# Scores of six chunks by their heads' rows, a switch for the causal mask of four chunks, and another order of the opening

## The chip, the cores and the metric

The kernel runs on one core of a Trainium2 chip. The metric is the device time of one launch in microseconds (us), as a median of several runs. The engines of the core are TensorE (PE), VectorE (DVE), ScalarE (ACT), GpSimd (POOL) and SyncE (SP), which issues the transfers. Each engine works through its own list of instructions in order.

## The reference

Two parts follow one another. The first is a recurrence with gates over 4 batches, 8 heads and 768 tokens, with heads of 40 numbers; its output, scaled by an output gate, is the input of the second, a feed-forward layer (FFN) on 3072 tokens of 320 numbers.

```python
for t in range(S):                                  # B, H, S, D = 4, 8, 768, 40
    m_new = np.maximum(f_gate[:, :, t] + m, i_gate[:, :, t])
    f_stab = np.exp(f_gate[:, :, t] + m - m_new)
    i_stab = np.exp(i_gate[:, :, t] - m_new)
    C = f_stab * C + i_stab * outer(vt, kt)         # one 40 x 40 state for each batch and head
    n = f_stab * n + i_stab * kt
    y[:, :, t] = sigmoid(o_gate) * (C @ qt) / np.maximum(np.abs(n @ qt), 1.0)
x = y.transpose(0, 2, 1, 3).reshape(3072, 320)
h = x @ w_in                                        # w_in 320 x 2048
g = np.maximum(h, 0.0) + alpha * np.minimum(h, 0.0)
out = g @ w_out                                     # w_out 2048 x 320
```

The weights `w_in` and `w_out` are stored as 64-bit floats.

## The kernel before

The tokens are cut into 24 chunks of 128. Within a chunk the recurrence is computed in closed form: products of q and k (the scores, `pS`), multiplied by the decay between the two tokens (`E`, zero where the second token is later than the first), times v (`pH`), plus what the state `C` of the chunks before gives (`pI`). A chunk's result, scaled by the gate (`og`, `xn`), is transposed to `x`. Two chunks make a group, and each of the 12 groups runs through the FFN: eight steps up (`ph`, 16 products each), a relu with slope on ACT and DVE (`g`), a split into a high part (`gh`, ACT) and a low part (`gl`, DVE or POOL), and eight steps down (`po`).

Chunks 0 to 5 are treated in another way than the rest. They make the opening, in which the weights are also fetched and turned from 64 bits into two parts of 32 bits each, high (`WH`, `OH`, `W`) and low (`WL`, `OL`). The opening ends when the first group's output is copied from `po` to `ob`. Behind it a written pattern of steps repeats for all further groups.

The order of the opening is written out by hand in the string `ORDER`. Each word is a step; the steps issue their instructions in this order, and `pin()` ties every engine, the queue of transfers on SP among them, to just this order. The words that matter here:

- `dq4`, `dv1`, `do1`, `dL4`: SP fetches q and k of chunk 4, v of chunks as stated, output gates, decay rows. Their tiles are `qn`, `kn`, `va`, `og`, `Lb`. The tiles of q and k are two each and serve the chunks by turns, so the load for chunk 4 needs chunk 2's transposes to be done.
- `qT4 qc4`, `kT4 kc4`: PE transposes q or k of chunk 4 into `pqk`, ACT copies it to `qf` or `kf`.
- `sp31`: PE spreads the decay of chunk 3's odd heads over a bank `pb` (L1064); `ex31`: ACT takes the exponential into `E`. `barred` (L100) adds, ahead of the spreading, a product with the mask `later`. `sc31`: the scores; `wg31`: DVE weighs them (L1101). `v3`: the product with v. `um3 uc3`: update of `C` (L221, L222). `gr3 gg3 gx3 gp3`: the gate (L439) and the product with it (L443).
- `i21d s x j h l`: a block of `w_in` (column block 2, row block 1; `wi2_1`); `d` loads it, `s` makes the upper bits on ACT (L855), then either `x` (one more pass on ACT, L865, and `j`, a join on DVE, L877) or `y` (a shift on DVE, L871, and `j`, L879). `h` is the high part on ACT (L887), `l` the low part on DVE and `p` the same on POOL (L891). `r` stands for the rest of `w_in` (`wr`), `o` for a block of `w_out` (`wo`).
- `U00 R00 S00 G00 K00` and `V01 r01 s01 g01 N01`: step up, relu, slope, high part, low part; with the capital letters DVE takes the low part, with V, small letters and N POOL does. `D00` is the step down, `Z0` the copy of the group's output.

Before, the scores of a chunk were computed for even and odd heads apart (`sc30`, `sc31`). A head's 40 rows lie at partitions 0 to 39 or 64 to 103 of the tiles. The products took all 104 rows, so the rows of the other head had to be zero in one operand: `kf` has two halves, each filled for one parity alone and set to zero elsewhere by four POOL memsets at the start.

```python
nc.tensor.matmul(ps[:, sl], qk[n][1][:R, par, sl], qk[n][0][:R, sl], start=True, stop=True)   # R = 104
```

Of the kernel before, what the change touches and what calls it, by code (L numbers as in the profile page):

```python
# [17 lines left out]
def kernel(ctx: ExitStack, tc: tile.TileContext, q, k, v, i_gate, f_gate, o_gate, w_in, w_out, alpha, out):  # L18
# [286 lines left out]
    kpads = []  # L305

    def padded_tiles():


        for K in kpads:  # L310
            nc.gpsimd.memset(K[64:R, 0], 0.0)
            nc.gpsimd.memset(K[:64, 1], 0.0)

# [3 lines left out]

    def padded(n):
        return kpads[(n + NDIR) % 2]

    def padded_copy(K, pk):
        nc.scalar.copy(K[:64, 0], pk[:64])
        nc.scalar.copy(K[64:R, 1], pk[64:R])
# [92 lines left out]
    def gated_steps(n, hv):  # L416
# [63 lines left out]
    def decays_of(n, par, Lb):  # L480

        b, c = divmod(n, NC)
        E = sb.tile([P, 512], F32, tag="E", name=f"E{n}_{par}", bufs=4)
        for p in range(NPR):
            h = 2 * p + par
            nc.scalar.activation(  # L486
                E[:, p * P : (p + 1) * P], Lb[:, h], AF.Exp, bias=bT[:, c, b * H + h : b * H + h + 1]
            )
        nc.gpsimd.affine_select(
            out=E, in_=E, pattern=[[0, NPR], [1, P]], base=0, channel_multiplier=-1,  # L490
            compare_op=ALU.is_ge, fill=0.0,
        )
        return E
# [162 lines left out]
    def first_stacks():  # L656
# [23 lines left out]
    XNP = range(2, NBF)  # L680
    KDP = range(1, 24)
    CP = range(6, 24)
    OBA = range(0)
    WIDE = 3 * VA
    ORDER = """warm18 kfz alT lf0z warm2 warm2 i00d i00s sca0 lf0a lf0b dq0 L0 sp01 qT0 dq1 alC li0 bj0 wt0 bTt kT0 i00x qc0 kc0 ewj
        i01d sca1 bTc ex01 sp00 sc00 qT1 wTt eeL wTc qc1 wd0 li1 lf1a lf1b kT1 sc01 i00j ex00 kc1 eTt Cz eTc sp11 ex11
        dv0 wg01 i01s wd1 L1 um0 uc0 i01x lpa um1 sp10 wg00 gma gmd ex10 i01j i00h fm1 ft1 sc11 do0 sc10 wg10 bj1 wtl
        blt ewl blc i00p o0d o0s r0d o0x gmm gmc r0s r0x v0 wg11 lpb lpc lpd uc1 dq2 qT2 o2d gr0 wlt og1 warm2 wlc r0j
        i11d lpe o0j i01h i01p gg0 qc2 dq3 gx0 gp0 kT2 v1 eel elt elc sp21 kc2 sc21 dL r0H ta1 gr1 gg1 sp20 ex21 qT3
        wg21 i10d dv1 r0h gx1 gp1 r0p r0L ex20 wd2 sc20 wg20 qc3 x0 x1 xa0 xd0 dq4 fm2 wd3 xa1 xd1 i10s F0 ft2 o2s o2y  # L690
        sp31 o0h ex31 kT3 o2j o2h i10y i10j um2 U00 o0l V01 kc3 R00 i11s uc2 i11y i11j o2l do1 i10h i10l sp30 r01 qT4
        qc4 ex30 S00 v2 sc31 i20d i20s ta2 gr2 i20x wg31 o1d og2 gg2 gx2 kT4 i20j kc4 sc30 wg30 G00 K00 i21d fm3 ft3
        s01 i20h o1s i20p i11h i11p o1x r2d o1j i21s i21x sc41 v3 um3 i21j uc3 ta3 dL4 U02 V03 r2s r2y o3d gr3 sc40
        ex41 fm4 R02 dq5 o1h o1l o4d g01 r2j N01 qT5 i21h i21p o3s S02 o3x G02 K02 dL5 wg41 i31d ft4 D00 wd4 dq6 o3j
        qc5 dv2 r2h r2p r03 ex40 o4s r2H D01 o4x gg3 s03 o3h o4j gx3 o5d gp3 wg40 i30d V04 r04 s04 dv3 o4h V05 gp2 x2
        x3 xa2 xd2 o6d do2 wd6 kT5 g04 r2P g03 o3l xa3 r05 o4l s05 v4 xd3 kc5 i31s ta4 N03 N04 i31y i31j i30s o5s o5x
        F1 V10 gr4 r10 um4 uc4 dL6 i30x um6 U11 ex50 R11 o5j s10 uc6 S11 ex51 g10 i31h dL7 i31p sc50 N10 i30j dq7 wg50
        U12 fm5 ft5 o5h sc51 wg51 v5 o7d R12 S12 ta5 D10 G11 K11 o6s o6x gr5 og3 gg5 G12 gx5 gg4 D11 K12 D12 i30h i30l
        gx4 U13 gp5 D02 tp0 do3 U06 o7s gp4 o5l o6j vp0 R13 tp1 g05 S13 G13 N05 K13 o7x o6h D13 vp1 o7j U07 tp2 tp3
        R06 S06 R07 x4 x5 xa5 xd5 D03 D04 D05 S07 o7h o7l G06 K06 o6l D06 xa4 xd4 G07 K07 D07 Z0"""  # L700
# [36 lines left out]
    class FeedForward:  # L737

        def __init__(self, g):
            self.g, self.x, self.done, self.named = g, x_tiles.pop(g), [], 0  # L740
# [4 lines left out]
        def up(self):  # L745
            for step in self.up_steps(self.g < 2):
                pass

        def up_steps(self, split=True):
            g, fp = self.g, self.named  # L750
            self.named += 1
# [34 lines left out]
            self.done.append((gh, gl))  # L786
# [179 lines left out]
    def first_group():  # L966
# [79 lines left out]
        def spread(n, par):  # L1046

            pb = psa(f"pb{n}_{par}")
            barred(pb)
            for p in range(NPR):  # L1050
# [3 lines left out]
                    start=False, stop=p == NPR - 1  # L1054
# [3 lines left out]
        def spread_later(n, par):  # L1058

            pb = psa(f"pb{n}_{par}")  # L1060
            barred(pb)
            for p in range(NPR):
# [3 lines left out]
                    LP[:, n % GC * P : (n % GC + 1) * P], start=False, stop=p == NPR - 1,  # L1066
# [5 lines left out]
        def decay(n, par):  # L1072
# [10 lines left out]
            E[n, par] = e  # L1083
# [4 lines left out]
        def scores(n, par):  # L1088
            if n >= GC:
                ps = psa(f"pS{n}_{par}")  # L1090
            elif n * par == 0:
                ps = ps_h.tile([P, 512], F32, tag="h", name=f"pS{n}_{par}")
            else:
                ps = ps_o.tile([P, 512], F32, tag="o1", name=f"pS{n}_{par}")
            for p in range(NPR):
                sl = slice(p * P, (p + 1) * P)
                nc.tensor.matmul(ps[:, sl], qk[n][1][:R, par, sl], qk[n][0][:R, sl], start=True, stop=True)
            pS[n, par] = ps
# [94 lines left out]
        def later_decays():  # L1193
# [29 lines left out]
            kfz=padded_tiles, Cz=zero_states,  # L1223
# [12 lines left out]
        def chunk_steps(n):  # L1236
# [61 lines left out]
        def named_ffn(g):  # L1298
# [68 lines left out]
```

## Time and profile before

| what | us |
|---|---|
| median of 3 runs (lowest, highest) | 465.4 (465.05, 465.82) |
| the profiled execution | 465.35 |
| its span | 463.6 |
| first group's output copied out from | 104.20 |

The profile is that of one execution; its span lies inside that execution's time, and 1.75 us lie around it. The engines' busy times are sums over all instructions; matmuls overlap each other, and their ends are modelled, so a busy PE may still lose time from one matmul's start to the next. A row of a group gives the line and the tiles, out<-in, with sizes, the count, the busy time and mean duration, and the idle time in front of them. A row of a timeline starts with the start time and the duration of a run of like instructions.

### The profile page before, as it was taken

Reading aid. Unit: us, or ns where it says so; the run is one execution under the profiler, and the core shown is the slowest. Engines: PE = TensorE matmul, PEld = TensorE weight load, DVE = VectorE, ACT = ScalarE, POOL = GpSimd, SP = SyncE. Lnnn points to the kernel's source line nnn. Section 1 sums busy time; section 2 is a strip of 40 time slices with the busy share of each in tenths; the row PEclk is TensorE's granted clock in tenths of the full one; section 3 lists DMA queues with packets and bytes.
Section 4 is the critical chain, followed back from the end, with each engine's and each line's share of the span. In section 5 each row is a group of like instructions: output and inputs, shape, how many; then the busy total and the mean of one; then the engine's idle time right before and its main releaser. Section 6 shows DMA issues by size and latency. Waiting matters only on the chain.

```text
span 463.6 us, 11813 instructions
## 1 busy us (share of the span) xinstructions
PE 452.8 (98%) x4366; PEld 442.0 (95%) x4366; DVE 329.8 (71%) x692; ACT 315.0 (68%) x707; POOL 308.4 (67%) x377
## 2 busy tenths in 40 slices
PE   8989989999999999999999999999999999999996
PEld 6879978999999999999999999999999999999996
DVE  4989998747776787886875887886776786764321
ACT  4899898676857858758856958757857858423331
POOL 8551674854698697588888598588888686324231
PEclk9999999999999999999999999999999999999999
DMA  9999994869775775888997686688796463020000
GB/s 184 177 221 252 277 252 118 175 122 190 151 182 147 138 184 160 137 174 173 158 187 176 122 197 168 133 166 180 153 206 156 107 154 90 1 84 15 28 2 28
DMA packets 186306, 68.67 MB, mean 148 GB/s; under 512 B 150234, under 2 KB 178506, under 8 KB 186250
## 3 DMA queue, kind: packets, MB, share of 16 engines
q1 hardware_dynamic: 186170, 67.83, 67.2%
q8 instruction: 34, 0.56, 0.5%
q14 instruction: 22, 0.18, 0.2%
q10 hardware_dynamic: 80, 0.11, 0.1%
HBM read 40.44 MB, written 7.57 MB: 104 GB/s over the span
## 4 chain that ended last, share of the span: by engine, by line
PE 83%; DVE 5%; DMA 5%; SPq 3%; ACT 3%; issue 1%; ACTq 0%; DVEq 0%
PE po L796 36%; PE ph L759 5%; PE ph L765 5%; PE ph L762 5%; PE ph L760 5%; PE ph L761 5%; PE ph L764 4%; PE ph L763 4%; PE ph L766 4%; PE pH L377 4%; PE pS L515 4%; DMA wi<-in_moe_w_in_dram 2%; DMA wr<-in_moe_w_in_dram 2%; PE pI L403 1%; PE pu L203 1%; DMA qn<-in_q_dram 1%
## 5 line engine op out<-in xcount | busy, mean ns | idle before, releaser
L785 POOL TENSOR_TENSOR gl<-g,gh 128x512 fp32r<-128x512 f32 x77 | 100.5, 1306 | 42.9 <-ACT gh L783 39.6
L796 PE MATMUL po<-OH,gh 128*128 128x320 f32 x368 | 110.7, 312 | 0.0
L796 PE MATMUL po<-OL,gh 128*128 128x320 f32 x368 | 109.3, 309 | 0.0
L769 ACT ACTIVATE g<-ph 128x512 f32<-128x512 f32 x96 | 57.1, 596 | 58.2 <-PE ph L766 56.0
L774 DVE SCALAR_TENSOR_TENSOR g<-g,oma,ph 128x256 f32<-128x256 f32 x156 | 66.8, 469 | 32.7 <-ACT g L769 32.3
L796 PEld LDWEIGHTS po<-OL,gh 128*128 128x128 f32 x368 | 69.2, 188 | 0.1
L796 PEld LDWEIGHTS po<-OH,gh 128*128 128x128 f32 x368 | 69.1, 188 | 0.0
L796 PE MATMUL po<-OH,gl 128*128 128x320 f32 x368 | 69.0, 309 | 0.0
L759 PE MATMUL ph<-XH,WH 128*128 128x256 f32 x192 | 57.2, 298 | 1.1 <-ACT wo L865 0.7
L796 PEld LDWEIGHTS po<-OH,gl 128*128 128x128 f32 x368 | 57.9, 188 | 0.0
L764 PE MATMUL ph<-XL,WH 128*128 128x256 f32 x192 | 54.3, 283 | 0.9 <-DVE XL L623 0.9
L765 PE MATMUL ph<-XL,WH 128*128 128x256 f32 x192 | 54.3, 283 | 0.0
L762 PE MATMUL ph<-XH,WL 128*128 128x256 f32 x192 | 54.3, 283 | 0.0
L760 PE MATMUL ph<-XH,WH 128*128 128x256 f32 x192 | 54.1, 282 | 0.0
L761 PE MATMUL ph<-XH,WL 128*128 128x256 f32 x192 | 54.1, 282 | 0.0
L364 ACT CAST E<-pS 128x512 bf16<-128x512 f32 x72 | 41.6, 582 | 18.0 <-DVE pS L361 14.0
L763 PE MATMUL ph<-XH,W 128*128 128x256 f32 x192 | 53.4, 278 | 0.2 <-POOL W L891 0.2
L766 PE MATMUL ph<-XL,W 128*128 128x256 f32 x192 | 53.4, 278 | 0.0
L783 ACT CAST gh<-g 128x512 fp32r<-128x512 f32 x77 | 46.5, 618 | 9.1 <-DVE g L774 6.6
L486 ACT ACTIVATE E<-Lb,bT 128x128 f32<-128x128 f32 x160 | 50.0, 392 | 0.0
L361 DVE TENSOR_TENSOR pS<-pS,E 128x512 f32<-128x512 f32 x36 | 24.8, 690 | 29.6 <-PE pS L515 26.2
L759 PEld LDWEIGHTS ph<-XH,WH 128*128 128x128 f32 x192 | 36.1, 188 | 2.0 <-ACT wo L865 0.9
(197 smaller groups left out, 1123.2 us busy)
## 6 DMA issues: line engine op xcount, KB each, us to landing
Lb<-L_d SPq DMA_DIRECT2D x20, 512.0 KB
wo<-in_moe_w_out_dram SPq DMA_DIRECT2D x8, 640.0 KB
wi<-in_moe_w_in_dram SPq DMA_DIRECT2D x8, 512.0 KB
qn<-in_q_dram SPq DMA_DIRECT2D x24, 160.0 KB
kn<-in_k_dram SPq DMA_DIRECT2D x24, 160.0 KB
va<-in_v_dram SPq DMA_DIRECT2D x24, 160.0 KB
og<-in_o_gate_dram SPq DMA_DIRECT2D x24, 160.0 KB
out_dram<-ob SPq DMA_DIRECT2D x11, 320.0 KB
```

What stands on the lines that cost most here:

```text
L759: nc.tensor.matmul(dst, WH[half][:, 0, hs], XH[:, 0], start=True, stop=False)
L760: nc.tensor.matmul(dst, WH[half][:, 1, hs], XH[:, 1], start=False, stop=False)
L761: nc.tensor.matmul(dst, WL[half][:, 0, hs], XH[:, 0], start=False, stop=False)
L762: nc.tensor.matmul(dst, WL[half][:, 1, hs], XH[:, 1], start=False, stop=False)
L763: nc.tensor.matmul(dst, W2[:, fs], X2, start=False, stop=False)
L764: nc.tensor.matmul(dst, WH[half][:, 0, hs], XL[:, 0], start=False, stop=False)
L765: nc.tensor.matmul(dst, WH[half][:, 1, hs], XL[:, 1], start=False, stop=False)
L766: nc.tensor.matmul(dst, W2[:, fs], X2L, start=False, stop=True)
L769: nc.scalar.activation(gt, ph, AF.Relu, scale=-1.0)
L774: nc.vector.scalar_tensor_tensor(out=y[:, e], in0=gt[:, e], scalar=oma[:, f : f + 1], in1=ph[:, e], op0=ALU.mult, op1=ALU.add)
L785: (nc.vector if split else nc.gpsimd).tensor_tensor(gl, y, gh.bitcast(F32), ALU.subtract)
L796: nc.tensor.matmul(po[j], x[:, e, j * P : (j + 1) * P], W[f // NB][:, f % NB], **ends)
```

## The change

There are four parts.

1. `scores(n)` computes all eight heads in one step, each with its own 40 rows, even and odd heads by turns into two banks. The step `sc{n}0` or `sc{n}1` that comes first does it, the other one does nothing. The padded tiles, their memsets and the second copy of k go away.
2. `BAR` names the chunks with a product with the mask; the others get a select on POOL (`causal`). `BAR` is `range(4)`: chunks 0 to 3 keep the product, and chunks 4 and 5 had a select before.
3. Numbers that set which engine takes a step: `OGP` (chunk 0's gate on POOL), `XNP` (chunks whose product with the gate is on POOL: 1 to 3, before 2 to 5), `CP` (chunks whose update of `C` starts on POOL: 1, 3 and 4 are added).
4. Another `ORDER`, and `first_turns`, a list of the two kinds of PSUM bank in the order in which the opening asks for them. In the new order seven of the thirteen blocks that took `x` take `y`, and four low parts `l` of `w_out` and two others become `p`. Two more steps up of group 1 and one of group 0 are written with small letters. The order of the loads is another one.

```diff
-    XNP = range(2, NBF)
-    KDP = range(1, 24)
-    CP = range(6, 24)
+    XNP = range(1, 4)
+    KDP = (1, 2, 3, 4, *range(6, 24))
+    CP = (1, 3, 4, *range(6, 24))
+    OGP = range(1)
+    BAR = range(4)
...
+    def open_gate_early(n):
+        if n in OGP:
+            sg = o_tiles[0][:, n]
+            nc.gpsimd.tensor_scalar(sg, sg, 1.0, None, ALU.add)
...
         if b == 0:
-            nc.vector.scalar_tensor_tensor(out=sg, in0=sg, scalar=1.0, in1=rb, op0=ALU.add, op1=ALU.mult)
+            if n in OGP:
+                nc.gpsimd.tensor_tensor(sg, sg, rb, ALU.mult)
+            else:
+                nc.vector.scalar_tensor_tensor(out=sg, in0=sg, scalar=1.0, in1=rb, op0=ALU.add, op1=ALU.mult)
...
-    def padded_copy(K, pk):
-        nc.scalar.copy(K[:64, 0], pk[:64])
-        nc.scalar.copy(K[64:R, 1], pk[64:R])
...
-                copy(qk[n][j][:R], pq[:R])
-            else:
-                padded_copy(qk[n][j], pq)
+                K = sb.tile([P, 2, 512], F32, tag="kS", name=f"kf{n}", bufs=2)[:, 0]
+                qk[n] = sb.tile([P, 512], F32, tag="qf", name=f"qf{n}"), K
+            copy(qk[n][j][:R], pq[:R])
...
             pb = psa(f"pb{n}_{par}")
-            barred(pb)
+            if n in BAR:
+                barred(pb)
...
-            E[n, par] = e
+            E[n, par] = e if n in BAR else causal(e)
...
+        def scores(n):
+            for par in range(2):
+                if n >= GC:
+                    pS[n, par] = psa(f"pS{n}_{par}")
...
+            for h in range(H):
+                p, par = divmod(h, 2)
+                sl, r = slice(p * P, (p + 1) * P), slice(64 * par, 64 * par + D)
+                nc.tensor.matmul(pS[n, par][:, sl], qk[n][1][r, sl], qk[n][0][r, sl], start=True, stop=True)
...
-                steps[f"sc{n}{par}"] = lambda par=par: scores(n, par)
+                steps[f"sc{n}{par}"] = lambda: (n, 0) in pS or scores(n)
...
-        wg21 i10d dv1 r0h gx1 gp1 r0p r0L ex20 wd2 sc20 wg20 qc3 x0 x1 xa0 xd0 dq4 fm2 wd3 xa1 xd1 i10s F0 ft2 o2s o2y
...
+        sc20 dq4 i20y i11s qT4 S00 sc31 sp30 gr2 i11y r01 qc4 i20j og2 wg31 G00 i11j ga2 r2d fm3
```

Three places show what the order moves. In the rows below a tile has its name and a running number; `qn0` is the tile that q of chunks 2 and 4 shares with chunk 0.

SP's queue before, from the load of chunk 4's q and k (`dq4`: the first two rows) to that of chunk 5's (the last two):

```order
L106 DMA qn0_75<-in_q_dram 128x8x40
L106 DMA kn0_77<-in_k_dram 128x8x40
L135 DMA og0_341<-in_o_gate_dram 128x8x40 x2
L845 DMA wi2_0_665<-in_moe_w_in_dram 128x1024
L928 DMA wo2_676<-in_moe_w_out_dram 128x2x640
L845 DMA wi2_1_699<-in_moe_w_in_dram 128x1024
L845 DMA wr2_719<-in_moe_w_in_dram 64x1024 x2
L126 DMA Lb4_755<-L_d_88 128x8x128
L928 DMA wo6_794<-in_moe_w_out_dram 128x2x640
L106 DMA qn1_76<-in_q_dram 128x8x40
L106 DMA kn1_78<-in_k_dram 128x8x40
```

SP's queue now, down to the load of chunk 4's q and k (the last two rows):

```order
L846 DMA wi1_0_416<-in_moe_w_in_dram 128x1024
L846 DMA wi2_0_457<-in_moe_w_in_dram 128x1024
L846 DMA wi1_1_485<-in_moe_w_in_dram 128x1024
L1264 DMA L_d_88<-g_L_131 32x768
L138 DMA og0_212<-in_o_gate_dram 128x8x40 x2
L846 DMA wi2_1_584<-in_moe_w_in_dram 128x1024
L929 DMA wo2_595<-in_moe_w_out_dram 128x2x640
L109 DMA qn1_76<-in_q_dram 128x8x40
L109 DMA kn1_78<-in_k_dram 128x8x40
L109 DMA qn0_75<-in_q_dram 128x8x40
L109 DMA kn0_77<-in_k_dram 128x8x40
```

Chunk 4's loads stand behind the gate, three weight blocks (`wi2_0`, `wi2_1`, `wo2`) and chunk 5's loads, all of which they had in front of before.

PE before, behind the first two steps up: one spreading, the transposes of chunk 4's q, chunk 2's product with v, and chunk 3's scores, odd heads first:

```order
L1064 MATMUL pb3_0_629<-LP_90,pick_91 128x128
L266 MATMUL pqk4_0_637<-ident_72,qn0_75 104x128 x4
L337 MATMUL pH2_651<-va1_80,E2_0_496 128x126
L337 MATMUL pH2_651<-va1_80,E2_1_476 128x126
L337 MATMUL pH2_651<-va1_80,E2_0_496 128x126
L337 MATMUL pH2_651<-va1_80,E2_1_476 128x126
L337 MATMUL pH2_651<-va1_80,E2_0_496 128x126
L337 MATMUL pH2_651<-va1_80,E2_1_476 128x126
L337 MATMUL pH2_651<-va1_80,E2_0_496 128x126
L337 MATMUL pH2_651<-va1_80,E2_1_476 128x126
L1097 MATMUL pS3_1_660<-qf3_509,kf1_134 128x128 x4
L266 MATMUL pqk4_1_681<-ident_72,kn0_77 104x128 x4
```

PE now, behind the second step up:

```order
L767 MATMUL ph0_1_610<-XL0_519,W2_73 128x256
L274 MATMUL pqk4_0_641<-ident_72,qn0_75 104x128 x4
L1099 MATMUL pS3_0_648<-qf3_483,kf3_482 128x128
L1099 MATMUL pS3_1_649<-qf3_483,kf3_482 128x128
L1099 MATMUL pS3_0_648<-qf3_483,kf3_482 128x128
L1099 MATMUL pS3_1_649<-qf3_483,kf3_482 128x128
L1099 MATMUL pS3_0_648<-qf3_483,kf3_482 128x128
L1099 MATMUL pS3_1_649<-qf3_483,kf3_482 128x128
L1099 MATMUL pS3_0_648<-qf3_483,kf3_482 128x128
L1099 MATMUL pS3_1_649<-qf3_483,kf3_482 128x128
L103 LDWEIGHTS ident_72
L103 MATMUL pb3_0_658<-later_92,ident_72 128x512
```

The eight products of chunk 3 stand together and go to two banks by turns; chunk 2's product with v has moved ahead of the two rows' step up, and the spreading behind the scores.

POOL now, where two low parts of `w_out` (`OL`) stand between low parts of `w_in`, a product with the gate, an update of `C` and a select:

```order
L892 TENSOR_TENSOR OL_105<-t_wo_357,OH_104 128x640
L892 TENSOR_TENSOR WL_103<-t_wi_0_597,WH_102 128x512
L438 TENSOR_TENSOR xn_664<-T_564,og_212 128x320
L892 TENSOR_TENSOR WL_703<-t_wi_0_607,WH_702 128x512
L892 TENSOR_TENSOR WL_103<-t_wi_1_639,WH_102 128x512
L218 TENSOR_TENSOR C_85<-C_87,gamB 104x336
L488 AFFINE_SELECT E_1_802<-E_1_802 128x512
L892 TENSOR_TENSOR OL_105<-t_wo_741,OH_104 128x640
```

Before, the two `OL` were steps of DVE, and so was the product that starts the update of `C`.

More of the change, by code (lines that the diff above doesn't have):

```diff
@@ L40 @@
     turns = ["b", "a"]
+    first_turns = list("abababababaabababbbabaababaabbaabbaabbaababbaababab")
     def psa(name, tag=None):
+        if tag is None and first_turns:
+            tag = first_turns.pop(0)
         if tag is None:
@@ L303, in shifted @@
         chunk[n] = (Q, K, None)
[L305 to L312, printed above, removed]
     def zero_states():
@@ L488, in decays_of, with causal @@
             )
+        return causal(E)
+    def causal(E):
         nc.gpsimd.affine_select(
@@ L739, in __init__ @@
         def __init__(self, g):
-            self.g, self.x, self.done, self.named = g, x_tiles.pop(g), [], 0
+            self.g, self.x, self.done = g, x_tiles.pop(g), {}
             if g == 1:
@@ L743, in __init__, with up_steps @@
                 self.po = [ps_a.tile([P, 512], F32, tag="b", name=f"po{g}_{j}")[:, :DM] for j in range(GC)]
[L745 to L751, printed above, removed]
+        def up_steps(self, fp, split):
+            g = self.g
             XH, XL, X2, X2L = self.x
@@ L1027, in by_token @@
             yield
-        for j in range(2):
-            kpads.append(sb.tile([P, 2, 512], F32, tag="kS", name=f"kf{j}", bufs=2))
         qk = {}
@@ L1053, in spread @@
                     pb[:, p * P : (p + 1) * P], ident[:, h : h + 1].broadcast_to([P, P]), L_all[:, n * P : (n + 1) * P],
-                    start=False, stop=p == NPR - 1
+                    start=n not in BAR, stop=n not in BAR or p == NPR - 1
                 )
@@ L1060, in spread_later @@
             pb = psa(f"pb{n}_{par}")
-            barred(pb)
+            if n in BAR:
+                barred(pb)
             for p in range(NPR):
@@ L1065, in spread_later @@
                     pb[:, p * P : (p + 1) * P], pick[:, h : h + 1].broadcast_to([3 * BH, P]),
-                    LP[:, n % GC * P : (n % GC + 1) * P], start=False, stop=p == NPR - 1,
+                    LP[:, n % GC * P : (n % GC + 1) * P], start=n not in BAR, stop=n not in BAR or p == NPR - 1,
                 )
@@ L1082, in decay @@
                 )
-            E[n, par] = e
+            E[n, par] = e if n in BAR else causal(e)
             yield
         pS = {}
[L1088 to L1098, printed above, removed]
+        def scores(n):
+            for par in range(2):
+                if n >= GC:
+                    pS[n, par] = psa(f"pS{n}_{par}")
+                elif n * par == 0:
+                    pS[n, par] = ps_h.tile([P, 512], F32, tag="h", name=f"pS{n}_{par}")
+                else:
+                    pS[n, par] = ps_o.tile([P, 512], F32, tag="o1", name=f"pS{n}_{par}")
+            for h in range(H):
+                p, par = divmod(h, 2)
+                sl, r = slice(p * P, (p + 1) * P), slice(64 * par, 64 * par + D)
+                nc.tensor.matmul(pS[n, par][:, sl], qk[n][1][r, sl], qk[n][0][r, sl], start=True, stop=True)
         def weigh(n, par):
@@ L1245, in chunk_steps @@
                 add(f"fm{n} ft{n}", lazily(lambda: state_part(n)))
+            steps[f"ga{n}"] = lambda: open_gate_early(n)
             add(f"gr{n} gg{n} gx{n} gp{n}", lazily(lambda: gated_steps(n, got["T" if n else "h", n])))
@@ L1306, in named_ffn @@
                 for tokens, split in (("URSGK", True), ("VrsgN", False)):
-                    add(" ".join(f"{x}{g}{fp}" for x in tokens), lazily(lambda split=split: ffs[g].up_steps(split)))
+                    add(" ".join(f"{x}{g}{fp}" for x in tokens), lazily(lambda fp=fp, split=split: ffs[g].up_steps(fp, split)))
                 steps[f"D{g}{fp}"] = lambda fp=fp: ffs[g].down(fp)
```

42 lines of the change are left out of this document (22 added, 20 removed).

## The prediction

> **What bounds the kernel now.** First the page: the span, then each engine's share.
>
> ```profile
> span 463.6 us, 11813 instructions
> PE 452.8 (98%) x4366; PEld 442.0 (95%) x4366; DVE 329.8 (71%) x692; ACT 315.0 (68%) x707; POOL 308.4 (67%) x377
> ```
>
> PE is busy for 98% of the span, so a gain needs less PE work or fewer of the few microseconds in which PE is idle. The profiled execution took 465.35 us: 463.6 of span and 1.75 around it. The median of the runs, 465.4 us, is the same within 0.05 us, and I add my sum to 465.35. Next the stretches, to see where those few are (PE, weight loads, DVE, ACT, POOL, granted clock, DMA share, GB/s).
>
> ```profile
> 0.00:10.00 10.00, 8.27 (x54) 6.36 (x54) 4.82 (x14) 4.21 (x6) 8.47 (x27) 1.00 0.99 171
> 10.00:20.00 10.00, 9.48 (x106) 8.56 (x104) 7.60 (x13) 8.99 (x28) 6.82 (x9) 1.00 1.00 211
> 20.00:30.00 10.00, 8.42 (x75) 7.32 (x73) 8.93 (x21) 8.63 (x18) 3.92 (x5) 1.00 1.07 241
> 30.00:40.00 10.00, 9.64 (x96) 8.69 (x95) 8.88 (x20) 9.40 (x24) 3.43 (x4) 1.00 0.84 159
> 40.00:50.00 10.00, 9.82 (x96) 9.38 (x96) 9.64 (x19) 9.80 (x21) 3.65 (x3) 1.00 1.09 295
> 34.90:66.00 31.10, 30.03 (x265) 29.02 (x260) 28.49 (x55) 28.43 (x61) 14.72 (x15) 1.00 1.04 261
> 66.00:104.30 38.30, 36.31 (x300) 35.27 (x299) 26.81 (x54) 29.17 (x65) 24.67 (x30) 1.00 0.70 150
> 104.30:463.60 359.30, 355.78 (x3537) 351.72 (x3534) 249.09 (x529) 231.27 (x520) 246.42 (x291) 1.00 0.62 134
> ```
>
> The diff touches only the opening, which ends when the first FFN group is copied out near 104.3 us. Behind that PE is busy for 355.78 of 359.30 us with work that the change leaves as it is, so what the opening gains or loses is carried to the end. In the opening, the DMA share is at 0.99 or above in all but one of the slices to 50 us: up to there transfers set the pace. From 34.9 to 66 PE (30.03 of 31.10), DVE (28.49) and ACT (28.43) are all close to full; PE is idle for 1.07 us there and 1.99 us behind it. The chain of waits says the same of the start:
>
> ```profile
> 14.25 8.14 DMA wr<-in_moe_w_in_dram
> 28.56 4.91 DMA qn<-in_q_dram
> ```
>
> Two transfers and the steps behind them carry the path up to the first up product. PE's own waits name DVE and ACT (total us, times, longest):
>
> ```profile
> PE ph L764 <- DVE XL L623: 0.9, 1, 0.9
> PE pb L100 <- DVE xn L443: 0.8, 1, 0.8
> PE pH L337 <- DVE E L1101: 0.8, 2, 0.6
> PE ph L759 <- ACT wo L865: 0.7, 1, 0.7
> ```
>
> **The scores by their heads' rows.** Before, a chunk's eight products use 104 rows with zeros in one operand; now they use 40 rows, at partitions 0 and 64 by turns, into two banks. PE's timeline of before (start, us, line, operation) has both shapes' nearest relatives:
>
> ```profile
> 17.80 1.99 PE L1097 MATMUL pS<-qf,kf 104*128 104x128 f32 x16
> 19.72 0.43 PE L1022 MATMUL ps_gb<-ident,g_WH 32*128 32x32 f32 x4
> 19.99 0.55 PE L1188 MATMUL pg<-g_gd,unit 32*104 32x192 f32 x2
> 34.51 0.51 PE L203 MATMUL pu<-va,kd 128*40 128x42 f32 x16
> 34.94 0.38 PE L759 MATMUL ph<-XH,WH 128*128 128x256 f32 x1
> 39.28 0.60 PE L266 MATMUL pqk<-ident,qn 128*104 128x128 f32 x4
> ```
>
> A chunk's sixteen records take 19.72 − 17.80 = 1.92 us from start to start, 120 ns each. If two products in different rows run side by side, the floor is half, 0.96 us; another floor is loading 128 columns of weights, which the four records of ps_gb do in 19.99 − 19.72 = 0.27 us, 67 ns each, so 1.08 us for sixteen. The pu products, packed by columns, need 34.94 − 34.51 = 0.43 us for sixteen, 27 ns each, and show that this PE does run neighbours together; they are small, though, so I stay with the nearer row: 1.2 us with the change into and out of the mode, a gain of 0.72 us for a chunk. Ends: 0 (nothing overlaps) and 0.96. Six chunks make 4.3 us, but the first three lie in the stretch that transfers pace; their 2.2 us turn into waiting. Chunks 3 to 5 lie behind: **−2.2 us** (0 to −2.9).
>
> The Trainium skill says on "TensorE: Matmul & The Clock Gate", Part 3 (packing small matmuls), that products in different row groups run together, four such in a third of the time; the same page's section on LDWEIGHTS prices a load by its columns alone, estimated from it 107 ns for 128 of them, which would leave sixteen records at 1.71 us and make the term −0.6 instead of −2.2. The ps_gb row, 67 ns, speaks against that second figure; no row shows row packing itself.
>
> **The mask.** The rows added in the code let a chunk leave out the product with the mask and take a select instead, but the set `BAR` holds chunks 0 to 3, so those keep their products, and 4 and 5 had selects before. POOL's list has as many selects as before. This part costs and brings nothing.
>
> **Work taken from ACT and DVE, put on POOL.** Rows of the opening (busy us, mean ns):
>
> ```profile
> L865 ACT ACTIVATE wo<-wo 128x640 uint32<-128x640 uint32 x7 | 5.6, 806 | 0.0
> L865 ACT ACTIVATE wi<-wi 128x512 uint32<-128x512 uint32 x5 | 3.4, 676 | 0.0
> L322 ACT COPY kf<-pqk 64x512 f32<-64x512 f32 x6 | 3.5, 577 | 0.4 <-PE pqk L266 0.4
> L891 DVE TENSOR_TENSOR OL<-t_wo,OH 128x640 fp32r<-128x640 f32 x8 | 7.0, 891 | 0.0
> L785 DVE TENSOR_TENSOR gl<-ph,gh 128x512 fp32r<-128x512 f32 x4 | 2.7, 683 | 0.7 <-ACT gh L783 0.7
> L221 DVE TENSOR_TENSOR C<-C,gamB 40x168 f32<-40x168 f32 x8 | 2.5, 318 | 0.1
> L871 DVE TENSOR_SCALAR t_wi<-t_wi 128x512 uint32<-128x512 uint32 x3 | 1.7, 574 | 0.0
> L891 POOL TENSOR_TENSOR WL<-t_wi,WH 128x512 fp32r<-128x512 f32 x6 | 8.2, 1371 | 1.6 <-ACT WH L887 1.5
> L785 POOL TENSOR_TENSOR gl<-g,gh 128x512 fp32r<-128x512 f32 x4 | 6.2, 1569 | 2.3 <-ACT gh L783 2.3
> L312 POOL MEMSET kf<- 64x512 f32 x2 | 1.0, 517 | 0.1
> ```
>
> ACT loses seven conversion passes (4 × 0.806 for wo, 2 × 0.676 for wi and one of wr, which has wi's size: 5.3 us) and six of its twelve kf copies (6 × 0.577 = 3.5; the six that stay read 104 partitions instead of 40 or 64): −8.8 us. DVE gains seven shifts in their place (7 × 0.574 = +4.0) and loses four low parts of w_out (4 × 0.891 = 3.6), two of W and WL (priced as gl, 1.4), three gl (2.0) and six half updates of C (1.9): −4.9 us. Chunk 0's gate goes to POOL and one of POOL's gate products comes to DVE, which I count as even for DVE. POOL loses four memsets (2.1) and gets the four low parts of w_out (1.371 × 640/512 = 1.7 each, estimated by size: 6.9), the two of W and WL (2.7), three gl (4.7), three full updates of C and one gate step net, which are smaller than WL's 128×512 and count 0.8 each, as an estimate by size (3.2): about +15 us, with POOL busy for 14.72 of 31.10 and 24.67 of 38.30 us in the two stretches. All this lies beside PE. What it can bring is the removal of waits: PE's idle 1.07 + 1.99 = 3.06 us behind 34.9, of which DVE and ACT are named in each of the rows above. With both relieved I take three quarters away: **−2.3 us** (0 to −3.1).
>
> **Against it, the loads.** The order of the loads on SP's queue changes, and one move matters: q of chunk 4 (qn0, step dq4) stood ahead of a gate load (og) and three loads of weights (wi2_0, wo2, wi2_1); now it stands behind all four and behind chunk 5's q and k. Added up from the order, 8.95 MB are ahead of it and in it; k follows. Before, by the GB/s column, 1.71 + 2.11 + 2.41 + 1.59 = 7.82 MB had moved by 40 us; the other 1.13 MB at 295 GB/s would take 3.8 us more: 43.8 us at the latest. But the slice with 159 GB/s holds an idle queue:
>
> ```profile
> 28.56 2.23 SPq L106 DMA_DIRECT2D qn<-in_q_dram  x1
> 34.22 0.37 SPq L106 DMA_DIRECT2D kn<-in_k_dram  x1
> SPq L106 <- POOL WL L891: 4.7, 1, 4.7
> ```
>
> From 30.8 to 34.2 SP issued nothing, since the load of k waited for POOL. In the new order no load of q or k stands at that place; the slice at 250 GB/s would have moved 0.9 MB more, so 8.95 MB by 40.9 us. I take **42.6** (ends 40.9 and 43.8). PE reached the transposes of chunk 4's q at 39.28 before, 4.3 us behind the first up product at 34.94. Now the value product of chunk 2 stands ahead of them (sixteen records of 112 ns, 1.8 us) and one spreading goes behind (0.6): +1.2 us, moved and not added, so PE gets there at 40.5 if the first up product starts where it did, and stands until 42.6. Scores of chunk 3 and all later up products are queued behind. **+2.1 us** (0.4 to 3.3). The first two chunks' q and k come first now, and v of chunk 1 moves ahead of q of chunk 2: the first up product may start earlier by what PE is idle from 20 us on, 1.58 and at most 0.36 us, or later by 0.8. The later start has two sources. DVE's gate product of chunk 0 now waits for two steps on POOL, and behind it in DVE's queue stand chunk 1's gate, the join of W's rest and chunk 2's weighting, for which the first x transposes and v of chunk 2 wait. And a chunk's scores take two banks at once, so a bank may come free late, as in the row of pb, where PE waited 0.8 us. An earlier start only lengthens the standing at chunk 4, so I count **0** (0 to +0.8).
>
> **Sum.** −2.2 − 2.3 + 2.1 + 0 = −2.4 us; 465.35 − 2.4 = 462.95, say 463.0.
>
> **Rivals.** *No overlap by rows.* If the sixteen records stay at 1.92 us, −2.2 falls away: −0.2, so 465.2. For it speaks that no row of this trace shows packing by rows, against it pu's 27 ns. The skill's LDWEIGHTS price is nearest to this rival.
>
> *POOL in DVE's way.* One pair of rows shows the danger (POOL's timeline, DVE's timeline, DVE's group of the same step):
>
> ```profile
> 52.53 1.76 POOL L785 TENSOR_TENSOR gl<-g,gh 128x512 fp32r<-128x512 f32 x1 [0.99 <-ACT gh L783]
> 53.07 1.77 DVE L879 SCALAR_TENSOR_TENSOR t_wr<-wr,t_wr 128x512 uint32<-128x512 uint32 x1
> L879 DVE SCALAR_TENSOR_TENSOR t_wi<-wi,t_wi 128x512 uint32<-128x512 uint32 x3 | 2.1, 692 | 0.1
> ```
>
> The same join takes 0.69 us elsewhere; beside POOL's subtraction it ended 0.55 us after that did, 1.08 us late. With POOL 15 us busier, five of twelve joins caught like this would cost DVE 5.4 us, more than the 4.9 it is relieved of. Then the −2.3 falls away, and where DVE was already close to full, the excess of 0.5 us comes on top: 465.35 − 2.2 + 2.1 + 0.5 = 465.75. By the Trainium skill, "SBUF — State Buffer", section on who interferes with whom, DVE operations with two SBUF inputs and POOL's reads take one lock in turn, and the loser waits the whole operation; the pair of rows agrees, with 1.08 us.
>
> *The load later still: slower.* If chunk 4's q lands at 46 instead of 42.6, PE stands 3.4 us longer and the sum is +1.0: 466.4. It decides from 45.0 us on, where the sum is zero. For it: transfers of q, k, v and the gates are in small pieces, and the DMA share is at its limit already; against: bytes alone give 43.8 with the old stall.
>
> *Everything in time.* If q lands before 40.5 and the waits go, −2.2 − 3.1 and up to −0.9 from an earlier start: 459.2.
>
> **How the numbers follow.** Chances: my sum 0.40, everything in time 0.17, no overlap 0.15, POOL in DVE's way 0.12, the late load 0.16. The likeliest gives 463.0, with its own range of 461 to 464.5. The runs of before spread by 0.17%, so 0.2%, 0.93 us, is what can be told from no change. Faster: 0.40 × 0.95 + 0.17 + 0.15 × 0.35 = 0.60. Slower: 0.16 and half of POOL's 0.12, with a hundredth for the rest: 0.23. Same: the other 0.17. The range leaves a tenth on either side: from 459.4, inside the best case, to 466.6, just past the late load.
>
> **What would show it.** The sixteen score records in about 1.2 us instead of 1.92 (0 gained if 1.9); PE idle before the transposes of chunk 4's q near 40 to 43 us, released by the transfer of qn; ACT some 9 us less busy before the first copy-out and POOL some 15 more; joins at 0.7 us when free and above 1.2 when caught; the first output copied near 102 instead of 104.2 us. The prediction is wrong if that copy comes later than 103.5, or if the stretch behind it is not 359 us long.

## The result

The changed kernel is slower: 468.78 us (468.4 to 469.08) against 465.23 for the kernel before on the same chip, a ratio of 1.008 with a 95% interval of 1.0068 to 1.0092. A second measurement on another chip gave 469.17 and 1.0090 (1.0072 to 1.0107). The forecast was 463.0 with a range of 459.4 to 466.6. The profiled execution has a span of 466.9 us.

```profile
span 466.9 us, 11801 instructions
PE 454.3 (97%) x4366; PEld 442.0 (95%) x4366; DVE 328.5 (70%) x684; ACT 307.7 (66%) x694; POOL 325.0 (70%) x386
```

ACT is relieved and POOL loaded as forecast. PE's busy time has not shrunk, but it counts records that take longer at a lowered clock, as the next rows show. The stretches of the opening (same columns as before) say where to look:

```profile
10.00:20.00 10.00, 10.00 (x105) 8.82 (x104) 6.67 (x13) 7.54 (x24) 7.00 (x9) 0.83 1.11 242
30.00:40.00 10.00, 9.15 (x99) 8.51 (x96) 8.64 (x17) 7.44 (x17) 6.44 (x7) 1.00 0.96 247
40.00:50.00 10.00, 7.09 (x45) 5.71 (x45) 7.08 (x15) 5.93 (x17) 2.95 (x3) 0.62 1.22 222
50.00:60.00 10.00, 10.00 (x93) 9.68 (x94) 7.26 (x13) 7.74 (x16) 7.22 (x8) 0.87 0.92 259
```

From 40 to 50 us PE is busy for 7.09 us with 45 matmul records, where it had 96 before. And the granted clock, 1.00 in every one of these stretches before, is 0.62 here, 0.87 in the next, and 0.83 from 10 to 20. The waits of PE and its timeline around 40 us:

```profile
PE pqk L274 <- DMA qn<-in_q_dram: 2.9, 1, 2.9
...
PE ps_gb L1023 <- ACT qf L1039: 0.9, 1, 0.9
```

```profile
40.13 0.28 PE L767 MATMUL ph<-XL,W 128*128 128x256 f32 x1
43.32 1.07 PE L274 MATMUL pqk<-ident,qn 128*104 128x128 f32 x4 [2.91 <-DMA qn<-in_q_dram]
44.32 2.08 PE L1099 MATMUL pS<-qf,kf 40*128 40x128 f32 x16
46.33 0.61 PE L103 MATMUL pb<-later,ident 128*128 128x512 bf16 x1
```

PE comes to the transposes of chunk 4's q at 40.4 and starts them at 43.32, when the transfer of `qn`, issued at 35.75, has landed. Then they take 1.07 us for what took 0.60 before, and the scores 2.08. Slices of one microsecond (PE busy, granted clock, DMA share, GB/s) show why:

```profile
41.00:42.00 1.00, 0.00 (x0) 1.00 1.48 136
42.00:43.00 1.00, 0.00 (x0) 0.68 1.51 163
43.00:44.00 1.00, 0.68 (x4) 0.50 1.18 183
...
51.00:52.00 1.00, 1.00 (x6) 0.50 0.69 119
52.00:53.00 1.00, 1.00 (x9) 0.70 0.81 246
53.00:54.00 1.00, 1.00 (x14) 1.00 0.80 274
```

While PE stands idle the granted clock falls from 1.00 to 0.50, and it stays there for nine microseconds after PE is at work again. The first group's output is copied out 3.72 us later than before (104.20), and later than the 103.5 that the prediction had named as the sign of being wrong:

```profile
107.92 0.89 DVE L830 COPY ob<-po 128x320 f32<-128x320 f32 x2 [1.85 <-PE po L797]
```

Span and copy-out moved by about the same, 3.3 and 3.7 us, so the stretch behind the opening is as long as it was: 466.9 − 107.92 = 359.0 us, before 463.6 − 104.20 = 359.4.

The profiled execution of the second measurement has the same place, with other sizes:

```profile
40.00:50.00 10.00, 6.30 (x41) 5.28 (x40) 6.53 (x14) 6.10 (x16) 2.22 (x3) 0.73 1.24 216
PE pqk L274 <- DVE t_wi L880: 3.7, 1, 3.7
```

The load is issued 1.1 us later (36.84), the transposes start at 44.31 after a wait of 3.7 us, and the clock is at half for 6.8 us, from 44.6, just after PE is at work again, to 51.4, and nowhere else. The view puts this wait down to a step of DVE that ended just then; the two loads exchanged, below, show that it is the load.

### The profile page after: what moved, and what is told of

Its sections match the earlier page's. It is cut to its first block, busy times and chain, and to the rows that moved or that the text cites. A ratio compares the mean times of both kernels' runs of the same rounds, so it can differ in the third digit from the quotient of the medians.

```text
span 466.9 us, 11801 instructions
## 1 busy us (share of the span) xinstructions
PE 454.3 (97%) x4366; PEld 442.0 (95%) x4366; DVE 328.5 (70%) x684; ACT 307.7 (66%) x694; POOL 325.0 (70%) x386
## 4 chain that ended last, share of the span: by engine, by line
PE 87%; ACT 3%; POOL 3%; DMA 3%; issue 2%; DVE 1%; SPq 0%; POOLq 0%
PE po L797 36%; PE ph L760 5%; PE ph L763 5%; PE ph L766 5%; PE ph L761 5%; PE ph L762 5%; PE ph L765 5%; PE ph L767 4%; PE ph L764 4%; PE pH L369 4%; PE pS L514 4%; DMA qn<-in_q_dram 2%; PE pu L211 1%; PE pI L395 1%; DMA wi<-in_moe_w_in_dram 1%
## 5 line engine op out<-in xcount | busy, mean ns | idle before, releaser
L786 POOL TENSOR_TENSOR gl<-g,gh 128x512 fp32r<-128x512 f32 x78 | 101.9, 1309 | 37.8 <-ACT gh L784 34.5
L775 DVE SCALAR_TENSOR_TENSOR g<-g,oma,ph 128x256 f32<-128x256 f32 x162 | 69.4, 469 | 32.5 <-ACT g L770 32.2
```

The lines of the kernel that those rows point to most:

```text
L775: nc.vector.scalar_tensor_tensor(out=y[:, e], in0=gt[:, e], scalar=oma[:, f : f + 1], in1=ph[:, e], op0=ALU.mult, op1=ALU.add)
L786: (nc.vector if split else nc.gpsimd).tensor_tensor(gl, y, gh.bitcast(F32), ALU.subtract)
```

## The experiments

All times are medians in us, ratios are against the kernel before, measured beside it on the same chip (464.87 to 465.12). Where single executions are told apart, it is by the mean of their granted clock: 3.41 us at half clock lower it by about 0.004 (3.41 × 0.5 / 463). First the late load was undone, filled, or left with an earlier start.

**Chunk 4's load ahead of two weight blocks.**

```diff
-        o0p ft2 o2j U00 i21d v2 o1d i10s dq5 ...   sc20 dq4 i20y i11s qT4
+        o0p ft2 o2j U00 dq4 i21d v2 o1d i10s dq5 ...   sc20 i20y i11s qT4
```

> The changed kernel with one word of the order moved: the load of chunk 4's q and k stands ahead of the fifth and sixth weight blocks (wi2_1, wo2) and of chunk 5's q and k again. Theory 'late load and clock': PE's 2.9 us wait for that transfer goes, and with it the ten microseconds at half clock behind it, up to 7.9 us in all; some of it turns into waits for DVE and ACT, so 461 to 464 us, with a granted clock of 1.00 from 40 to 56 us. Rival 'POOL's added work': DVE and POOL are what is late in this stretch, the freed time turns into waits for them, and the time stays above 467.5.

Measured 465.36, ratio 1.000 (0.9986 to 1.0014). No trace of it shows the clock; two kernels below that have the load in time do ("Both" and "The two loads exchanged"). The move of one word gives the whole loss back, so POOL's added work is not what made the kernel slower. It does not reach the 461 to 464 that the gain in PE time would have given.

**Idle products in the wait.**

```diff
-        i20y i11s qT4 S00 sc31
+        i20y i11s warm26 qT4 S00 sc31
```

> The changed kernel, with 26 idle products of 256 columns (107 ns each, 2.8 us) put on PE right ahead of the transposes that wait for chunk 4's q. Nothing else moves; the transfer lands as late as it did. Theory 'late load and clock': the wait is filled, the clock stays at 1.00, and up to 5 us (ten microseconds at half clock) come back: 464 to 466.5. Rival 'the wait alone': the half clock lay beside work of DVE and ACT that sets the pace there, and the time stays within 0.8 us of the changed kernel's 468.8.

Measured 467.81, ratio 1.0065 (1.0039 to 1.0091): between the two expectations, and not clearly better than the changed kernel, whose interval it overlaps. In the profiled execution (469.19) the clock stayed at 1.00 from 40 to 60 us, but it fell earlier instead (0.83 from 20 to 30), everything behind was 2 us later, and the load landed at 45.20. The executions differ widely: three with a mean clock of 0.999 or 1.000 took 465.47 to 466.12, the other nine, at 0.996 or less, 467.36 to 471.35. So where the wait was filled and the clock fell nowhere, most of the loss was gone, with the load as late as before; the median does not show it.

**The first copies first.**

```diff
-        alT kT0 warm2 i00s qc0 dv0 li0 lf0b alC i01d kc0 L0
+        alT kT0 warm2 qc0 dv0 li0 lf0b alC i01d kc0 i00s L0
```

> The changed kernel, with ACT's copies of chunk 0's q and k ahead of its first weight conversion, which waits for a transfer until 7.83 us. Both theories: PE's 0.9 us wait at 8 us goes, and the half clock from 11 to 15 us with it (1.9 us of PE time). Theory 'late load and clock': PE only reaches the late load sooner and stands there longer, so the time stays at 467.8 to 469. Rival 'PE paces the start too': 2 us and more come back, 466.8 or less.

Measured 468.37, ratio 1.0063 (1.0042 to 1.0083), as the late load has it: with the load still late, PE waited 3.9 us for it instead of 2.9. What is won ahead of the late load is spent in front of it.

**Both.** The two edits above together, the load's move and the first copies.

> Both edits: chunk 4's load early and the first copies first. Theory 'late load and clock': no half clock anywhere, and what PE gains at the start is no longer lost at the load: 459.5 to 463, at least 1 us below the kernel with the early load alone. Rival 'transfers pace the start': the same as with the early load alone, within 0.6 us.

Measured 465.23, ratio 1.0002 (0.9989 to 1.0015): the same as with the load alone, so the rival held. In the profile, of an execution 0.9 us below the median (464.30), the copy-out starts at 103.17, but PE still waits where DVE and ACT are late. This kernel, with neither long wait, was the ground for the next four.

**All 104 rows again.**

```diff
-                sl, r = slice(p * P, (p + 1) * P), slice(64 * par, 64 * par + D)
+                sl, r = slice(p * P, (p + 1) * P), slice(0, R)
```

> The kernel with both edits (early load, first copies first; 465.2 us), whose scores again take all 104 rows for each of the eight products, so that no two run side by side. The other head's rows are not zero here, so the scores are sums over two heads: only the time counts. It undoes the row packing alone. Theory 'the packing's gain turns into waits': six chunks get 0.8 us longer on PE, of which PE then waits less for DVE, ACT and transfers; 465 to 466.5 us. Rival 'PE paces the opening': the 5 us come back in full, 469 to 470.5.

Measured 464.83, ratio 0.9994 (0.9985 to 1.0004). Taking the packing away costs nothing. The packing itself works; the changed kernel's timeline has a chunk's sixteen records at full clock from 18.29 to the next group at 19.38, 1.09 us instead of 1.92:

```profile
18.29 1.16 PE L1099 MATMUL pS<-qf,kf 40*128 40x128 f32 x16
19.38 1.12 PE L389 MATMUL pI<-C,qf 104*128 104x126 f32 x8
```

So 0.83 us for a chunk are saved, five for all, and not one of them is in the time: PE is not what sets the pace of the opening once it waits for others. Part of it may be the clock. With all rows every execution had a mean clock of 0.999 or 1.000; with the packing one of twelve had, and the other eleven had 0.993 to 0.996, which is one or two stretches of 3.41 us at half clock. The runs do not tell how much of the packing's gain went that way and how much in waiting.

**POOL's new work back on DVE.**

```diff
-    XNP = range(1, 4)
-    CP = (1, 3, 4, *range(6, 24))
-    OGP = range(1)
+    XNP = range(2, NBF)
+    CP = range(6, 24)
+    OGP = ()
-    ... o0p ... o1p ... o3p ... o4p ...
+    ... o0l ... o1l ... o3l ... o4l ...
```

> The kernel with both edits (465.2 us), with most of the work that the change gave to POOL put back on DVE: the four low parts of w_out, chunk 0's gate, the updates of C for chunks 1, 3 and 4, and the products with the gate as before. Theory 'POOL in DVE's way': joins and lows on DVE are no longer caught, 462.5 to 464.3. Rival 'DVE needs the relief': DVE is close to full between 30 and 66 us and gets about 5 us more to do, 466 to 469.

Measured 466.11, ratio 1.0021 (1.0007 to 1.0035), 0.9 us above the ground (465.23; the intervals touch). So the moves to POOL bring a little or nothing; they do not cost.

**The mask by selects after all.**

```diff
-    BAR = range(4)
+    BAR = range(0)
```

> The kernel with both edits (465.2 us), with the set of chunks that keep the product with the mask made empty, so that chunks 0 to 3 take selects on POOL instead: eight products of some 0.22 us leave PE, and eight selects of 0.66 us come to POOL, each between the exponential and the weighing. Theory 'POOL is late': the weighing waits for POOL behind low parts and gates, 466 to 469. Rival 'PE paces the opening': 1.8 us less on PE, 463.4 to 464.6.

Measured 468.58, ratio 1.0078 (1.0058 to 1.0098): slower by 3.4 us, as the theory 'POOL is late' had it, and that is the part of the change that the set `BAR` leaves out. The selects took 722 ns each, PE waited 2.4 us for weighed scores, and the clock fell to 0.66 from 20 to 30 us (in the profiled execution, 470.12, the slowest of six).

**Idle products near 19 us.**

```diff
-        dq3 warm2 wtl i00p
+        dq3 warm9 wtl i00p
```

> The kernel with both edits (465.2 us), with seven more idle products (0.75 us) where PE waits 0.64 us for ACT at 19.7 us and falls to half clock from 21 to 25 us. Theory 'the clock': no half clock there, so up to 1.9 us come back: 463.2 to 464.6. Rival 'transfers and DVE pace the start': the clock stays up and the time is the same within 0.5 us.

Measured 465.16, ratio 1.0009 (0.9995 to 1.0024): the clock stayed at 1.00 to 60 us, and the time did not move. But the half clock had not gone, it came later, from 61.3 to 64.7 us:

```profile
60.00:70.00 10.00, 10.00 (x84) 9.87 (x85) 6.21 (x15) 8.76 (x21) 9.70 (x10) 0.83 0.81 185
```

Ten of the twelve executions have a mean clock of 0.995 or 0.996, as most had without the added products. So this run does not show what a half clock near 20 us costs.

**The two loads exchanged.** Only the order of chunk 4's and chunk 5's load in the changed kernel is turned round; nothing else differs.

```diff
-        v2 o1d i10s dq5 kc3 R00 ...   sc20 dq4 i20y i11s qT4
+        v2 o1d i10s dq4 kc3 R00 ...   sc20 dq5 i20y i11s qT4
```

> The changed kernel with the loads of chunk 4 and chunk 5 exchanged, so that chunk 4's q lands some 2.3 us earlier than in the changed kernel, near 41 us, and PE waits 0.5 to 1 us for it instead of 2.9. Theory 'late load and clock': so short a wait leaves the clock at 1.00 from 42 to 52 us, and most of the 3.5 us come back: 464.6 to 466. Rival 'the queue as a whole': chunk 5's load is now late instead and PE waits there, 467 to 469.

Measured 465.03, ratio 1.0002 (0.9991 to 1.0012), against the unchanged one beside it:

> The changed kernel as it is, for comparison on the same chip: 468 to 469 us.

which measured 469.17, ratio 1.0090 (1.0072 to 1.0107). In the stretches of the kernel with the exchange PE has 99 records from 40 to 50 us, and the clock stays up:

```profile
40.00:50.00 10.00, 9.02 (x99) 7.79 (x99) 9.26 (x18) 9.47 (x22) 5.46 (x5) 1.00 1.18 227
50.00:60.00 10.00, 9.65 (x76) 9.21 (x75) 9.86 (x18) 8.66 (x17) 8.69 (x9) 1.00 0.91 262
```

The transposes of chunk 4's q started at 39.86, after 0.51 us that the view puts down to DVE and not to the transfer. Only two loads changed places, and the whole loss is gone: the late load is its cause. DVE and ACT are both near full (9.26 and 9.47, then 9.86 of 10), as they were before.

**PE busy, load late.**

> The changed kernel with its late load, but with PE kept busy: first copies first, nine idle products instead of two near 19 us, and 36 idle products (3.9 us) right ahead of the transposes that wait for chunk 4's q. The load lands as late as before; only the clock is kept up. Theory 'the half clock is most of the loss': 465.2 to 466.8. Rival 'the wait itself is the loss': the later steps start as late as they did, 467.8 to 469.

Measured 468.21, ratio 1.0064 (1.0040 to 1.0089), near the rival. It decides nothing: in the profile the clock fell to 0.66 from 20 to 30 us, in front of the place, PE came there only at 42.5, and the transposes started at 46.45, behind the products; how much of that was the load and how much the products, it does not show. Its two executions with a clock of 0.999 and 1.000 took 466.18 and 466.52, the other four 468.14 to 470.15.

**Another place for an x transpose.**

```diff
-        gx3 o3h x2 dq6 gp3 r2P V04 ex40
+        gx3 o3h dq6 gp3 r2P V04 x2 ex40
```

> The kernel with both edits, the nine idle products near 19 us, and the first x transpose of the second group put behind a step up, where PE waited 1.6 us for ACT near 58 us. Theory 'PE's waits and the clock': both remaining falls of the clock go, 463 to 464.3. Rival 'DVE paces 40 to 66 us': DVE is full there, and the time stays at 464.6 to 465.6.

Measured 465.15, ratio 1.0003 (0.9990 to 1.0016). The wait of 1.6 us went, and others for DVE (two, 1.7 us together) and POOL (1.4 us) came in its place.

**A busy hold-up.** To the kernel with the exchange, 27 idle products are added ahead of the transposes, with the load in time:

```diff
-        i20y i11s qT4 S00 sc31
+        i20y i11s warm27 qT4 S00 sc31
```

> The kernel with the two loads exchanged (465.0 us, clock 1.00), with 27 idle products (2.9 us) ahead of the transposes of chunk 4's q: PE is held up there for as long as the late load held it, but is busy, and the load is in time. It measures the hold-up without the half clock. Theory 'the half clock is most of the loss': 465 to 466.5, since DVE and ACT pace that stretch and PE makes up for it. Rival 'the wait is the loss': 2.5 to 3.5 us more, 467.5 to 468.5.

Measured 466.44, ratio 1.0029 (1.0016 to 1.0042). The transposes start when they did in the changed kernel, at 43.32, and the clock is up:

```profile
40.36 3.12 PE L168 MATMUL warm<-ident 128*128 128x256 bf16 x27
43.32 0.60 PE L274 MATMUL pqk<-ident,qn 128*104 128x128 f32 x4
...
40.00:50.00 10.00, 9.83 (x109) 8.65 (x109) 8.62 (x18) 8.61 (x21) 4.38 (x4) 1.00 1.17 215
```

The hold-up of 2.9 us costs 466.44 − 465.03 = 1.4 us in the median, and not even that is the hold-up alone. One execution of the twelve had a mean clock of 1.000 and took 464.71, no longer than without the hold-up; five at 0.996 took 465.71 to 466.23, and six at 0.991 to 0.993 took 466.66 to 467.83. The profiled one is of the last kind (467.62): its clock is at half from 11.1 to 14.5 us and again from 62.3 to 65.7, at the end of a wait of 3.0 us for ACT:

```profile
60.00:70.00 10.00, 7.31 (x52) 7.32 (x53) 5.52 (x10) 7.69 (x17) 7.24 (x8) 0.83 0.89 211
PE p L604 <- ACT qf L1039: 3.0, 1, 3.0
```

The changed kernel loses 468.78 − 465.03 = 3.7 us (4.1 in the second measurement). What is left, at least 2.3 to 2.7 us, is the difference between a busy and an idle PE at the same start, and it comes with the seven to ten microseconds at half clock. That the clock, and not something else that goes with an idle PE, makes this difference is argued from the executions told apart here and with the idle products; no run sets the clock alone.

**Shifts back on ACT.** In the kernel with the exchange, four blocks, and then seven, take ACT's second pass again instead of DVE's shift.

```diff
-        i10y  i20y  i11y  i21y
+        i10x  i20x  i11x  i21x
```

> The kernel with the two loads exchanged (465.0 us), with four weight blocks of the stretch from 34 to 60 us (two each of the second and third column block of w_in) converted with ACT's pass again instead of DVE's shift: DVE loses 4 x 0.57 us, ACT gets 4 x 0.68. Theory 'DVE paces 40 to 66 us': 463.5 to 464.5. Rival 'ACT is as full there': no change or slower, 464.8 to 466.

> The same with three further blocks (the first of w_out and both of the rest of w_in), seven in all, as many as the change had moved from ACT to DVE. Theory 'DVE paces 40 to 66 us': 463 to 464.3. Rival 'ACT is as full there': 465 to 467.

Measured 467.12 (1.0041, 1.0027 to 1.0055) and 465.96 (1.0028, 1.0011 to 1.0044). Neither is faster than with the shifts on DVE (for seven blocks the intervals touch), so DVE alone does not pace this stretch. ACT is full with four blocks more, and PE idle:

```profile
40.00:50.00 10.00, 7.15 (x80) 5.90 (x80) 7.70 (x16) 10.00 (x24) 4.71 (x5) 1.00 1.22 219
```

None of the kernels beats the one before beyond its interval; the best, with the load in time, are level with it.

## Why the prediction was wrong

The forecast was −2.4 us, measured were +3.6 (468.78 − 465.23), 6.0 us apart. With the load in time the kernels are level with the one before (465.03 to 465.36), so the two gains, 4.5 us in the sum, came to nothing; and the late load cost 3.7 us where the sum had 2.1.

**The late load: seen, and priced too low.** The step "+2.1 us (0.4 to 3.3)" had the place, the queue and the mechanism. The load was there at 43.3, between the ends 40.9 and 43.8 and near the upper; PE was there at 40.4, where 40.5 was forecast; the wait was 2.9 us instead of 2.1 (3.7 in the second profile, where the load came at 44.3, just past the upper end). What failed is what the wait costs. The sum counted it as its own length. Measured, 2.9 us of standing costs at most 1.4 us when PE is busy meanwhile, and 3.7 when it is idle and the granted clock halves. The view that gave the prediction its clock column showed 1.00 everywhere, with no wait of PE above 0.93 us behind its first products, and I took the clock as given when I added a wait of more than twice that. The rival "the load later still" had a loss from a landing at 46 us, 466.4 in all; the load landed earlier and the loss was larger, so that was the wrong reason.

By the Trainium skill, "TensorE: Matmul & The Clock Gate", Part 1 (the clock gate), the array's clock is halved after an idle window of about 3.4 us and restored after a busy one. The trace agrees that an idle PE is throttled to one half, but here a gap of 2.91 us was enough, and full clock came back only 9 us after the work did (7 in the second profile).

**The packing: right in size, wrong in place.** "−2.2 us (0 to −2.9)" was made of 0.72 us for each of three chunks; measured were 0.83. The step that failed is that chunks 3 to 5 lie where PE sets the pace. Without the packing the time is the same (0.9994), so all six chunks' savings turned into waiting and perhaps half clock, where I had said waiting, and of the first three only. The rival "no overlap by rows" gave 465.2, about what the kernels with the load in time take, but for another reason: the records did overlap, 1.09 us for sixteen, and its mechanism is refuted.

**The relief of DVE: not there.** "−2.3 us" rested on DVE and ACT being relieved by 4.9 and 8.8 us. Over the first 104 us, before and with the load in time and the first copies first, the two rows of each are (PE, weight loads, DVE, ACT, POOL):

```profile
0.00:34.00 34.00, 29.81 (x258) 25.31 (x259) 24.92 (x56) 25.27 (x61) 21.76 (x42) 1.00 1.00 198
34.00:104.00 70.00, 66.94 (x572) 64.81 (x573) 55.70 (x109) 58.50 (x127) 39.97 (x46) 1.00 0.84 198
```

```profile
0.00:34.00 34.00, 31.43 (x278) 26.50 (x279) 24.22 (x55) 22.58 (x56) 24.31 (x43) 0.95 1.07 218
34.00:104.00 70.00, 65.34 (x570) 62.48 (x569) 58.42 (x103) 52.98 (x117) 51.77 (x51) 1.00 0.79 183
```

ACT went from 83.8 to 75.6 us (−8.2) and POOL from 61.7 to 76.1 (+14.4), both as forecast. DVE did not go from 80.6 to 75.7; it went up to 82.6, with fewer instructions (165 and 158). Of the 82.6, 0.8 us is the first group's copy-out, which begins at 103.17 here and only at 104.20 before; up to the copy it is 81.8, still 1.2 more. The same operations got longer, first before, then with the early load:

```profile
L877 DVE SCALAR_TENSOR_TENSOR t_wo<-t_wo,wo 128x640 uint32<-128x640 uint32 x7 | 8.1, 1162 | 0.4 <-ACT wo L865 0.2 <-POOL xn L443 0.2
L871 DVE TENSOR_SCALAR t_wo<-t_wo 128x640 uint32<-128x640 uint32 x1 | 0.5, 494 | 0.4 <-ACT t_wo L855 0.4
```

```profile
L892 DVE TENSOR_TENSOR OL<-t_wo,OH 128x640 fp32r<-128x640 f32 x4 | 5.6, 1398 | 0.0
L878 DVE SCALAR_TENSOR_TENSOR t_wo<-t_wo,wo 128x640 uint32<-128x640 uint32 x3 | 4.3, 1435 | 0.5 <-POOL WL L892 0.5
L872 DVE TENSOR_SCALAR t_wo<-t_wo 128x640 uint32<-128x640 uint32 x5 | 3.7, 734 | 0.1
```

The low parts that stayed on DVE take 1.40 us instead of 0.89, the joins 1.44 instead of 1.16, and a shift 0.73 instead of 0.49. In the changed kernel one sees such a shift beside POOL (POOL's timeline, then DVE's):

```profile
34.91 1.29 POOL L892 TENSOR_TENSOR W<-t_wr,W 64x512 fp32r<-64x512 f32 x1 [1.38 <-ACT W L888]
35.23 1.33 DVE L872 TENSOR_SCALAR t_wo<-t_wo 128x640 uint32<-128x640 uint32 x1
```

In the kernel with the load in time, the one low part of `w_out` on DVE with no operation of POOL beside it, at 38.79, took 0.82 us; the three beside POOL's, from 87.43 on, took 1.40, 1.42 and 1.95.

The rival "POOL in DVE's way" therefore had its mechanism right: the relief of 4.9 us was eaten. Its price and its source were not. With most of POOL's new work back on DVE the time was 0.9 us longer, not shorter (the intervals touch), and DVE was busy for 85.9 us up to the copy, 4.0 more than with that work on POOL. Its eight low parts still took 1.32 us each:

```profile
L892 DVE TENSOR_TENSOR OL<-t_wo,OH 128x640 fp32r<-128x640 f32 x8 | 10.4, 1315 | 0.0
```

So the moves did relieve DVE, and a good part of what ate the relief is not the work that was moved. It comes with the rest of the change, likely with where the new order puts DVE's steps beside POOL's; no run tests that alone. None of it caused the loss, which went with the load.

**The start and the mask.** That an earlier or later start does not matter ahead of the late load held (the first copies first: no gain). With the load in time it still brought nothing. The mask's part was inert as stated, and would have cost 3.4 us.

**The chances.** Slower had 0.23, and no case reached 468.8. The missing case was a clock that falls behind a wait. Nor was there a case in which both gains fail at once, which would have been 465.35 + 2.1 = 467.45: the rivals were priced one at a time.

## What to carry to other kernels

A load that is moved behind others in a queue is priced by when it lands against when its engine comes for it, and for TensorE the wait can cost more than itself: here 3.7 us for 2.9 of waiting, against at most 1.4 when PE was kept busy. In a stretch in which transfers, DVE and ACT are near full, shorter matmuls buy only idle time; test it by making them long again before counting them. Work moved from DVE to POOL shortens DVE by less than its length where the steps that stay run beside POOL's; here DVE's busy time went up by 1.2 us where 4.9 us, as estimated, had been taken away. And look at the granted clock of every execution, not only of the profiled one: a median can mix executions with and without a fall of the clock.

## What was not expected of the hardware

The clock falls and rises on a grid of 3.41 us. In slices of half a microsecond, every stretch of half clock in the traces that show the clock is 3.41, 6.83 or 10.24 us long, one, two or three times 3.41. Within one execution the falls lie whole multiples of 3.41 us apart: in the changed kernel from 11.64 and from 42.36 us, nine times 3.41, and with seven shifts back on ACT from 11.47, 45.61 and 76.33 us, ten and nine times. From one execution to the next the grid lies elsewhere: the changed kernel's second profile falls at 44.61, which is not on the first one's. So the same wait can meet the grid early or late.

What makes the clock fall is not settled by these runs. One gap of 2.91 us halved it for ten microseconds. At 8.1 us a gap of 0.91 us in the changed kernel was followed by half clock from 11.6 to 15.1 us, while before a gap of 0.93 us at 66.9 was followed by none:

```profile
12.00:13.00 1.00, 1.00 (x6) 0.50 1.10 263
```

With four shifts back on ACT, PE was idle for 2.85 of ten microseconds in several short pieces, and the clock stayed at 1.00. PE's busy share in the 3.41 us in front of a fall lay between 0.00 (the first copies first, from 39.58) and 0.81 (both edits, from 17.43), while stretches of the changed kernel's grid with 0.70 (from 28.71) and 0.67 (from 66.25) had no fall behind them. So the busy share of these records does not decide it, and how long a gap must be, and at what phase, no run here tells.
